# A spectral filter beside a token MLP on one core: the even half first, five buffer pairs in freed memory, single filter rows by small early transfers

## The chip, the cores and the metric

The kernel runs on one core of a Trainium2 chip. The metric is the device time of one launch in microseconds (us), the median of three runs. Beside it stands one profiled execution, from which all rows of the profile come.

## The reference

Two branches read the input `A_x` and its gate mixes them. The shapes are S = 2048 rows, D = 512 columns, F = 1792, all in bf16. `B_x` isn't read.

```python
x = A_x
g = sigmoid((x * gate_w).sum(-1, keepdims=True))
X = rfft2(x.astype(float32)) * (A_w_r + 1j * A_w_i)      # 2048 x 257
a = irfft2(X, s=(2048, 512)).astype(bfloat16)
h = layernorm(x)                                         # over D
u = gelu(einsum("bsd,sf->bdf", h, B_w1) + B_b1)          # tanh form
b = (einsum("bdf,fs->bds", u, B_w2) + B_b2).transpose(0, 2, 1)
return g * a + (1 - g) * b
```

## The kernel before

The function adds tasks (engine, estimated duration, emitting function, what it reads and writes, priority) to a planner, class `Plan`. `Plan.order` runs a list schedule over them by its own cost estimates and priorities, and the instructions are then emitted in that order. So each engine's order is fixed when the kernel is built, and it stands in the order of the program: an engine that waits holds up everything behind it. The entry `pk` of a transfer holds the number of its row pieces, their bytes, and on how many DMA engines the planner puts it.

Rows of `x` are numbered j = 4q + r; a tile of 128 rows belongs to each j.

*MLP.* Layer norm on VectorE and ScalarE (L473 to L531) makes `h`. The first product (L699, 224 matmuls of 512 columns) runs in an order of its own over 14 blocks of F, its GELU is L713 on ScalarE. The second product (L977, 14 matmuls for each j) is TensorE's filler until the end. For j under 14 ScalarE evicts it with gate and bias (L993); for the last two VectorE adds it in the tail (L1019).

*Spectral branch*, a two-dimensional transform in stages:

1. Along S: radix-4 sums of `x` on VectorE (L539 to L546), matmuls with `ta` (L556 to L559), evictions (L562), radix-4 sums (L569 to L576). The result is `X`, in two halves, index `lt`: even frequencies (0) and odd ones (1).
2. `radix4` (L595 to L608) on both halves: the odd half first, then the even half, whose first column is mended by a small chain (L620 to L638) and written at L646.
3. Along D: matmuls with `tb` (L664 to L667), evictions to `B` (L671), for the even half first.
4. Filter: `bfly` (L814, L815), multiplication by `W` (L822), `comb` (L827, L828), `ob` (L834 to L836); the Nyquist line apart (`nyq`, L795 to L798, and transfers through `s9` and `s8`). `W` and its mirror image are prepared before: `wt` is flipped by matmuls (L751), evicted (L755, L764), and the edges are taken at `wprep` (L771 to L775).
5. Inverse: `radix4` again (L595 to L611), matmuls (L883 to L890), evictions (L896, L898), folds (L906 to L919).
6. Last transform: for each j five matmuls (L957 to L961), an eviction to `eo` with the gate (L967), then for each pair a fold through `es` back into `eo` (L982 to L988) and an addition to the MLP's rows (L1007). `NEO` and `NES`, 2 each, are the pairs of buffers; a pair comes free after its L1007.

*Loads.* Nearly all are issued by SyncE (L310) in the planned order. `ld_W` loads, for the real and the imaginary filter, rows into `W` and `wt` in six transfers; eight single rows come in one transfer to one partition of `xp`, and `special` (L447 to L451) copies them on ScalarE to their places after that. `gw`, the gate's weights, is loaded ahead of the first `ld_W`; L724 multiplies `x` by it and L729 sums the product.

Of the kernel before, what the change touches and what calls it, by code (L numbers as in the profile page):

```python
# [23 lines left out]
L = 256  # L24
WL = 258
# [112 lines left out]
class Plan:  # L138
# [11 lines left out]
    def add(self, eng, dur, emit, reads=(), writes=(), prio=0.0, alloc=(), free=(), pk=None, after=()):  # L150
        t = Task()
        t.eng, t.dur, t.emit, t.prio = eng, dur, emit, prio
        t.alloc, t.free, t.pk = tuple(alloc), tuple(free), pk
        t.users, t.end, t.ready = [], None, 0.0
        deps = set(after)
        for k in reads:
            if k in self.last_w:
                deps.add(self.last_w[k])
            self.readers.setdefault(k, []).append(t)
        for k in writes:  # L160
            if k in self.last_w:
# [81 lines left out]
def tt(n):  # L243
    return 0.07 + n / 1920.0
# [19 lines left out]
def tiny(k):  # L264
    return 0.09 * k + 0.06
# [3 lines left out]
def kernel(  # L269
# [14 lines left out]
    V, A, T = nc.vector, nc.scalar, nc.tensor  # L284
# [7 lines left out]

    pool = ctx.enter_context(tc.tile_pool(name="sb", bufs=1))
    psum = ctx.enter_context(tc.tile_pool(name="ps", bufs=1, space=bass.MemoryType.PSUM))
    NEO, NES = 2, 2

    def sb(shape, dt, tag, bufs=1):
        return pool.tile(shape, dt, tag=tag, name=tag, bufs=bufs)
# [2 lines left out]
        return psum.tile(shape, dt, tag=tag, name=tag, bufs=bufs)  # L301

    NB = {"acc": 4, "fa": 2, "fb": 2}
    caps = {"wa": 1, "wb": 2, "xf": 2, "eo": NEO, "es": NES, **NB}
    pl = Plan(caps)
    add = pl.add
    t = {}

    def dma(out_ap, in_ap, eng=None):
        (eng or nc.sync).dma_start(out=out_ap, in_=in_ap)  # L310
# [34 lines left out]
    a0 = add("SP", 0.6, alloc_first, writes=["warm", "xs", "eps"], prio=-9)  # L345
# [82 lines left out]

    wsrc = (A_w_r, A_w_i)

    def ld_W(comp, pr):
        v = wsrc[comp].rearrange("(e c k) l -> c e k l", e=4, k=4)
        z = wsrc[comp].rearrange("(e h i n k) l -> n h k i e l", e=4, h=2, n=2, k=2)
        wz = lambda: t["xp"][0:1, 2048 + 8 * WL * comp:2048 + 8 * WL * (comp + 1)].rearrange("p (j l) -> p j l", j=8)
        for n, (key, dst, src, pk) in enumerate((
                ("wz", lambda: wz()[:, :, 0:257], wsrc[comp].rearrange("(u j w) l -> w u j l", u=1, j=8)[0], (8, 514, 8)),
                ("u0", lambda: t["wt"][0:64, comp, 0, :, 0:257], z[0, 1, 0], (256, 514)),
                ("u2", lambda: t["wt"][64:128, comp, 0, :, 0:257], z[1, 1, 0], (256, 514)),
                ("u1", lambda: t["wt"][:, comp, 1, :, 0:257], v[:, :, 3, :], (512, 514)),
                ("w0", lambda: t["W"][0:64, comp, 0, :, 0, 0:257], z[0, 0, 0], (256, 514)),  # L440
                ("w2", lambda: t["W"][64:128, comp, 0, :, 0, 0:257], z[1, 0, 0], (256, 514)),
                ("w1", lambda: t["W"][:, comp, 1, :, 0, 0:257], v[:, :, 1, :], (512, 514)))):
            add("SP", 0.5, lambda dst=dst, src=src: dma(dst(), src), writes=[(key, comp)], prio=pr + 0.1 * n, pk=pk, after=[a0])

        def special():
            W, u, w = t["W"], t["wt"], wz()
            A.copy(u[0:1, comp, 0, 0:2, 0:257], w[:, 5:8:2, 0:257])  # L447
            A.copy(u[0:1, comp, 0, 2, 0:257], w[:, 6, 0:257])
            A.copy(u[0:1, comp, 0, 3, 0:257], w[:, 0, 0:257])
            A.copy(W[0:1, comp, 0, 2:4, 0, 0:257], w[:, 1:4:2, 0:257])  # L450
            A.copy(t["wn"][:, comp, 0:257], w[:, 4, 0:257])  # L451
        add("ACT", 2.2, special, reads=[(k, comp) for k in ("wz", "u0", "u1", "u2", "w0", "w1", "w2")], writes=[("W", comp), ("wt", comp)], prio=4.5)

    for comp in range(2):
        ld_W(comp, 17 + 8 * comp)
        if comp == 0:
            load_wb(1)

# [179 lines left out]
        V.tensor_add(fx[:, 3, 1], sd[:, 1, 0, 1], sp[:, 2, 1])  # L638
    add("DVE", tiny(12), sp1, reads=["sp"], writes=["fx"], prio=0)

    for lt in (1, 0):
        pr = 3.0 if lt else 3.1
        radix4(lambda lt=lt: t["X"][:, lt].rearrange("p r c j l -> p r c (j l)"),
               lambda: t["xp"][:, 0:2048], lambda: t["st"][:, 0:2048], "xs", "st",
               dk + ([] if lt else ["sp"]), [("Z", lt, 0), ("Z", lt, 1)], pr, False)
    add("DVE", 0.15, lambda: V.tensor_copy(t["X"][:, 0, :, :, :, 0], t["fx"][:]), reads=["fx"],  # L646
        writes=[("Z", 0, 0), ("Z", 0, 1)], prio=3.1)

    def tbl(kind, c):
        tb = t["tb"]  # L650
# [290 lines left out]
    def tbuf(j):  # L941
        if "tb_" not in t:
            t["tb_"] = sb([P, NJ, 2, L], BF16, "x")
        return t["tb_"][:, j]

    LATE = 14
    groups = [range(0, 4), range(4, 8), range(8, 12), range(12, 14), range(14, 15), range(15, 16)]
    for grp in groups:
        for j in grp:
# [12 lines left out]
            add("PE", mm(*[129] * 5), i3, reads=[("z", 0), ("z", 1), "tg"], writes=[("i3", j)], prio=4, alloc=[tag])  # L962

            def i3ev(j=j):
                if j % 2 == 0:
                    t["eo", j // 2] = sb([P, 2, 2, L], BF16, "eo", NEO)
                A.activation(t["eo", j // 2][:, j % 2], t["i3", j][:], ActF.Copy, scale=t["g"][:, j:j + 1])  # L967
# [22 lines left out]

            if j < LATE:
                def yev(j=j):
                    A.activation(tbuf(j).rearrange("p h d -> p (h d)"), t["y", j, 0][:], ActF.Identity, bias=t["ombb2"][:, j:j + 1],  # L993
                                 scale=t["omg"][:, j:j + 1])
                add("ACT", act(512, 2), yev, reads=[("y", j, 0), "omg"], writes=[("o", j)], prio=1, free=["acc"], after=gates)
                if j % 2 == 0:
                    continue

                def es(j=j, fold=fold, quart=quart):
                    s, e = sb([P, 2, 4, P], BF16, "es", NES)[:], t["eo", j // 2]  # L1000
                    fold(e[:].rearrange("p j h d -> p (j h) d"), quart(e[:]), s)
                add("DVE", tiny(1) + 4 * tt(512), es, reads=[], writes=[("eo", j - 1), ("eo", j)], prio=4, alloc=["es"], free=["es"])

                def fin(j=j):
                    tbuf(j)
                    o = t["tb_"][:, j - 1:j + 1]
                    V.tensor_add(o, o, t["eo", j // 2][:])  # L1007
                add("DVE", tt(1024), fin, reads=[("eo", j - 1), ("eo", j)], writes=[("o", j - 1), ("o", j)], prio=4, free=["eo"])
            else:
                def es(j=j, fold=fold, quart=quart):  # L1010
                    e, s = t["eo", j // 2][:, j % 2], sb([P, 2, 4, P], BF16, "es", NES)[:, :, 0:2]
                    V.tensor_scalar_add(e[:, 0, 0:129], e[:, 0, 0:129], t["ombb2"][:, j:j + 1])
                    fold(e, quart(tbuf(j)[:, None]), s)
                add("DVE", tiny(1) + 4 * tt(256) + 0.15, es, reads=[("eo", j), "omg"], writes=[("o", j)], prio=4, alloc=["es"], free=["es", "eo"] if j % 2 else ["es"], after=gates)

                for n, cs in enumerate(parts):
                    def fin(j=j, n=n, cs=cs):
                        o = tbuf(j).rearrange("p h d -> p (h d)")[:, cs]
                        V.scalar_tensor_tensor(o, t["y", j, n][:, cs], t["omg"][:, j:j + 1], o, op0=Alu.mult, op1=Alu.add)  # L1019
                    add("DVE", d1(cs.stop - cs.start) + 0.1, fin, reads=[("y", j, n), "omg", ("o", j)], writes=[("of", j, n)], prio=1,  # L1020
                        free=[("acc", "fa")[n]])
# [42 lines left out]
```

## Time and profile before

| | us |
|---|---|
| median of three runs | 136.37 (135.94 to 136.87) |
| the profiled execution, its time | 136.38 |
| its span, first to last instruction | 134.5 |
| TensorE busy | 124.2 (92%) |
| VectorE busy | 112.4 (84%) |
| ScalarE busy | 88.9 (66%) |

The granted TensorE clock was 0.998 in the mean. The costliest groups are the second product (L977: 30.8 and 23.9 us) and the first (L699: 28.6, 16.9 and 9.4 us). TensorE's busy time is modelled, and a matmul that follows another is shown as overlapping it: a 512-column one lasts some 0.37 us by its row and follows its neighbour after about 0.22. Engines stand as PE (TensorE), DVE (VectorE), ACT (ScalarE) and SP (SyncE); SPq and ACTq are their queues of issued transfers.

### The profile page before, as it was taken

How to read it: one execution, taken by the hardware profiler on the slowest of the kernel's cores; microseconds unless marked ns; L12 is line 12 of the kernel's file. 1: busy time of each engine (PE TensorE's matmuls, PEld its weight loads, DVE VectorE, ACT ScalarE, POOL GpSimd, SP SyncE). 2: the span in 40 equal slices, each digit the busy share in tenths (PEclk: the TensorE clock that was granted, in tenths of full speed). 3: DMA queues.
4: the chain of work that ended last, by engine and by line, in shares of the span. 5: the costliest groups of instructions: out<-in, count | busy, mean ns of one | idle time of the engine just before them, and what ended most of it. 6: DMA issues, size and time to landing. Idle time of an engine off the chain costs nothing.

```text
span 134.5 us, 2134 instructions
## 1 busy us (share of the span) xinstructions
PE 124.2 (92%) x758; PEld 70.9 (53%) x771; DVE 112.4 (84%) x259; ACT 88.9 (66%) x185; POOL 0.2 (0%) x4
## 2 busy tenths in 40 slices
PE   6899999998999799999999999999999999999920
PEld 2345555554454475654454545555777576555810
DVE  2899999899999969309999999999769739797990
ACT  3798694979999599899991072223699375749300
POOL 0000000000000000000000000000000000000000
PEclk9999999999999999999999999999999999999999
DMA  4999999999999999980019500000000000214331
GB/s 125 330 352 364 358 373 345 314 175 237 327 266 185 325 410 409 401 328 10 0 17 392 217 0 0 7 0 2 0 0 5 0 0 0 104 55 161 156 117 41
DMA packets 17215, 23.22 MB, mean 173 GB/s; under 512 B 1040, under 2 KB 14644, under 8 KB 17204
## 3 DMA queue, kind: packets, MB, share of 16 engines
q1 hardware_dynamic: 16772, 22.63, 53.3%
q10 hardware_dynamic: 432, 0.46, 1.0%
q8 instruction: 6, 0.10, 0.3%
q14 instruction: 5, 0.04, 0.1%
HBM read 20.97 MB, written 2.10 MB: 172 GB/s over the span
## 4 chain that ended last, share of the span: by engine, by line
PE 42%; DMA 28%; DVE 13%; SPq 8%; ACT 4%; issue 2%; DVEq 0%; ACTq 0%
PE acc L977 21%; PE acc L699 12%; DMA wa<-in_B_w_dram 9%; SPq L310 8%; DMA gw<-in_gate_w_dram 8%; DMA W<-in_A_w_i_dram 6%; DMA wb<-in_B_w_dram 4%; ACT eo L967 3%; DVE eo L987 2%; DVE es L984 2%; DVE x L1007 2%; DVE es L983 2%; DVE eo L988 2%; PE fb L883 1%; PE fb L667 1%
## 5 line engine op out<-in xcount | busy, mean ns | idle before, releaser
L977 PE MATMUL acc<-gl,wb 128*128 128x512 bf16 (+1 forms) x124 | 30.8, 372 | 0.2
L699 PE MATMUL acc<-h,wb 128*128 128x512 bf16 x124 | 28.6, 379 | 0.5 <-ACT gl L713 0.4
L977 PE MATMUL acc<-gl,wa 128*128 128x512 bf16 (+1 forms) x94 | 23.9, 372 | 0.1
L993 ACT ACTIVATE x<-acc,ombb,omg 128x512 bf16<-128x512 f32 x14 | 10.7, 780 | 18.1 <-PE acc L977 18.1
L977 PEld LDWEIGHTS <-wb 128*128 128x128 bf16 x136 | 15.1, 114 | 10.7 <-DMA wb<-in_B_w_dram 0.8
L699 PEld LDWEIGHTS <-wb 128*128 128x128 bf16 x128 | 12.5, 98 | 14.0 <-DMA W<-in_A_w_r_dram 0.7
L699 PE MATMUL acc<-h,wa 128*128 128x512 bf16 x61 | 16.9, 379 | 1.0 <-DVE h L503 0.9
L977 PEld LDWEIGHTS <-wa 128*128 128x128 bf16 x102 | 11.3, 114 | 8.0 <-issue 0.2
L699 PEld LDWEIGHTS <-wa 128*128 128x128 bf16 x96 | 9.3, 98 | 9.9 <-issue 1.2
L562 ACT CAST X<-fa 128x512 bf16<-128x512 f32 x16 | 9.0, 580 | 2.5 <-PE fa L559 2.5
L473 DVE BATCH_NORM_STATS2 stats<-x 128x6 f32<-128x512 bf16 x13 | 8.9, 681 | 1.6 <-DMA x<-in_A_x_dram 1.6
L729 ACT ACTIVATE x<-x 128x512 bf16<-128x512 bf16 x16 | 9.9, 626 | 0.0
L967 ACT ACTIVATE eo<-fa,g 128x512 bf16<-128x512 f32 x8 | 5.5, 688 | 6.4 <-DVE x L1007 4.1
L699 PE MATMUL fb<-h,wa 128*128 128x512 bf16 x32 | 9.4, 379 | 0.0
L713 ACT ACTIVATE gl<-acc,b1f 128x512 bf16<-128x512 f32 x12 | 8.0, 691 | 1.4 <-PE acc L699 1.2
L531 ACT ACTIVATE h<-x,nmr,rstd 128x512 bf16<-128x512 bf16 x9 | 7.3, 814 | 1.5 <-DVE nmr L528 1.5
L967 ACT ACTIVATE eo<-fb,g 128x512 bf16<-128x512 f32 x8 | 5.5, 688 | 0.0
L982 DVE COPY es<-eo 128x8 bf16<-128x8 bf16 (+1 forms) x9 | 1.6, 182 | 4.4 <-ACT eo L967 4.3
L477 ACT ACTIVATE rstd<-mv,eps 128x1 f32<-128x1 f32 x16 | 4.7, 296 | 0.5 <-DVE rstd L527 0.4
L671 ACT CAST B<-fa 128x512 bf16<-128x512 f32 x8 | 4.8, 598 | 0.3 <-PE fa L667 0.3
L724 DVE TENSOR_TENSOR x<-x,gw 128x2048 bf16<-128x2048 bf16 x4 | 4.9, 1220 | 0.1
L671 ACT CAST B<-fb 128x512 bf16<-128x512 f32 x8 | 4.8, 601 | 0.0
(177 smaller groups left out, 240.5 us busy)
## 6 DMA issues: line engine op xcount, KB each, us to landing
wb<-in_B_w_dram SPq DMA_DIRECT2D x8, 512.0 KB, 8.0
wb<-in_B_w_dram SPq DMA_DIRECT2D x4, 1024.0 KB, 6.9
wa<-in_B_w_dram SPq DMA_DIRECT2D x3, 1024.0 KB, 9.4
wa<-in_B_w_dram SPq DMA_DIRECT2D x2, 768.0 KB, 6.8
out_dram<-x SPq DMA_DIRECT2D x3, 512.0 KB, 2.9
x<-in_A_x_dram SPq DMA_DIRECT2D x2, 512.0 KB, 6.7
wa<-in_B_w_dram SPq DMA_DIRECT2D x2, 384.0 KB
rot<-dft_ti SPq DMA_DIRECT2D x1, 736.5 KB, 7.4
```

What stands on the lines that cost most here:

```text
L310: (eng or nc.sync).dma_start(out=out_ap, in_=in_ap)
L473: V.bn_stats(out=t["stats"][:, j, :], in_=t["x"][:, j // 4, j % 4, :])
L531: add("ACT", act(512, 2), lambda j=j: A.activation(t["h"][:, j // 4, j % 4, :], t["x"][:, j // 4, j % 4, :], ActF.Identity, bias=t["nmr"][ ...
L562: add("ACT", act(512), lambda r=r, dq=dq: A.copy(t["X"][:, :, r, :, dq, :], t["pa", r, dq][:]), reads=[("pa", r, dq)], writes=[("X", r, dq ...
L671: A.copy(t["B"][:, lt, e, 2 * c:2 * c + 2, :].rearrange("p s (i b) -> p s i b", b=4), t["pb", lt, e, c][:].rearrange("p s b i -> p s i b"))
L699: T.matmul(t["u", ft][:], lhsT=w[:, j // 4, j % 4, c * P:(c + 1) * P], rhs=t["h"][:, j // 4, j % 4, :], start=(j == jorder[0]), stop=(j == ...
L713: gelus.append(add("ACT", act(512, 1), lambda ft=ft: A.activation(t["gl"][:, ft, :], t["u", ft][:], ActF.Gelu_apprx_tanh, bias=t["b1f"][:, ...
L724: add("DVE", tt(2048), lambda r=r: V.tensor_mul(t["x"][:, :, r, :], t["x"][:, :, r, :], t["gw"][:, None, :].to_broadcast([P, 4, D])), read ...
L729: A.activation(t["x"][:, q, r, :], t["x"][:, q, r, :], ActF.Copy, accum_out=t["glog"][:, 4 * q + r:4 * q + r + 1])
L967: A.activation(t["eo", j // 2][:, j % 2], t["i3", j][:], ActF.Copy, scale=t["g"][:, j:j + 1])
L977: T.matmul(t["y", j, n][:, cs], lhsT=w[:, o, 512 * q + r:512 * q + 512:4], rhs=t["gl"][:, ft, cs], start=(ft == 0), stop=(ft == NFT - 1))
L993: A.activation(tbuf(j).rearrange("p h d -> p (h d)"), t["y", j, 0][:], ActF.Identity, bias=t["ombb2"][:, j:j + 1], scale=t["omg"][:, j:j + 1])
```

## The change

Three edits, all in the main function.

- *Even half first.* The second stage runs `radix4` for the even half first and writes its mended column right after it. The priorities of the inverse `radix4` change so that the even half's stays ahead of the odd half's by less. Since the planner orders all engines, matmuls of the first product move about the later stages too.
- *Buffers.* `eo` and `es` are no longer tiles of their own. One tile `E` takes the memory of tag `X` (which `zz` held before): five pairs for evictions, one for the fold's intermediate, two (`ob`, `NOB`) for the fold's result. A pair now comes free after its fold; the addition reads `ob`.
- *Filter rows.* The eight-row transfers and `special` go. Each filter has five small transfers, of four, two, one, one and one rows, straight to partition 0 of `W`, `wt` and to `wn`. Their priorities put them early in the queue, between the loads of `x`, `w1` and `ta`. The two large transfers that had covered partition 0 start at partition 1: 63 rows in place of 64. A task without an instruction (`NOP`) ties the eleven loads to the readers.

In the changed program the ten small transfers stand on SyncE as follows: `w1` row 1 (half), small, `ta` row 1, `w1` row 1 (half), six small, `x` row 2, small, `ta` row 2, `w1` row 2, two small, `flip`, the two biases, `x` row 3.

```diff
-    NEO, NES = 2, 2
+    NEO, NOB = 5, 2
...
-    caps = {"wa": 1, "wb": 2, "xf": 2, "eo": NEO, "es": NES, **NB}
+    caps = {"wa": 1, "wb": 2, "xf": 2, "eo": NEO, "ob": NOB, **NB}
...
-    def ld_W(comp, pr):
...
-                ("wz", lambda: wz()[:, :, 0:257], wsrc[comp].rearrange("(u j w) l -> w u j l", u=1, j=8)[0], (8, 514, 8)),
-                ("u0", lambda: t["wt"][0:64, comp, 0, :, 0:257], z[0, 1, 0], (256, 514)),
...
-                ("w0", lambda: t["W"][0:64, comp, 0, :, 0, 0:257], z[0, 0, 0], (256, 514)),
...
-        def special():
...
-            A.copy(u[0:1, comp, 0, 0:2, 0:257], w[:, 5:8:2, 0:257])
-            A.copy(u[0:1, comp, 0, 2, 0:257], w[:, 6, 0:257])
-            A.copy(u[0:1, comp, 0, 3, 0:257], w[:, 0, 0:257])
-            A.copy(W[0:1, comp, 0, 2:4, 0, 0:257], w[:, 1:4:2, 0:257])
-            A.copy(t["wn"][:, comp, 0:257], w[:, 4, 0:257])
+    def ld_W(comp, pr, early):
...
+                (lambda: W()[0:1, 0, :, 0, 0:257].rearrange("p (a b) l -> p a b l", a=2), few, (4, 514, 4)),
+                (lambda: u()[0:1, 0, 0:2, 0:257], w.rearrange("(c w) l -> w c l", c=4)[256:257, 2:4], (2, 514, 2)),
+                (lambda: u()[0:1, 0, 2, 0:257], w[1536:1537, :], (1, 514, 1)),
+                (lambda: u()[0:1, 0, 3, 0:257], w[0:1, :], (1, 514, 1)),
+                (lambda: t["wn"][:, comp, 0:257], w[1024:1025, :], (1, 514, 1)),
+                (lambda: u()[1:64, 0, :, 0:257], z[0, 1, 0, 1:64], (252, 514, 9)),
...
+                (lambda: W()[1:64, 0, :, 0, 0:257], z[0, 0, 0, 1:64], (252, 514, 9)),
...
+        add("NOP", 2.0, lambda: None, reads=keys, writes=[("W", comp), ("wt", comp)])
...
-        ld_W(comp, 17 + 8 * comp)
+        ld_W(comp, 17 + 8 * comp, [2.3 + 1.1 * comp + 0.3 * n for n in range(5)])
...
-    for lt in (1, 0):
-        pr = 3.0 if lt else 3.1
+    for lt in range(2):
+        pr = 3.0 + 0.1 * lt
...
-        writes=[("Z", 0, 0), ("Z", 0, 1)], prio=3.1)
+        writes=[("Z", 0, 0), ("Z", 0, 1)], prio=3.0)
...
-        pr = 3.25 + 0.2 * lt
+        pr = 3.35 + 0.05 * lt
...
+    def epair(k):
+        if "E" not in t:
+            t["E"] = sb([P, 8192], BF16, "X")
+        return t["E"][:, 1024 * k:1024 * k + 1024].rearrange("p (j h d) -> p j h d", j=2, h=2)
+
+    def espair():
+        return t["E"][:, 1024 * NEO:1024 * NEO + 1024].rearrange("p (k m d) -> p k m d", k=2, m=4)
...
-                if j % 2 == 0:
-                    t["eo", j // 2] = sb([P, 2, 2, L], BF16, "eo", NEO)
-                A.activation(t["eo", j // 2][:, j % 2], t["i3", j][:], ActF.Copy, scale=t["g"][:, j:j + 1])
+                A.activation(epair(j // 2 % NEO)[:, j % 2], t["i3", j][:], ActF.Copy, scale=t["g"][:, j:j + 1])
...
-                    s, e = sb([P, 2, 4, P], BF16, "es", NES)[:], t["eo", j // 2]
-                    fold(e[:].rearrange("p j h d -> p (j h) d"), quart(e[:]), s)
+                    e = epair(j // 2 % NEO)
+                    fold(e.rearrange("p j h d -> p (j h) d"), quart(epair(NEO + 1 + j // 2 % NOB)), espair())
...
-                    V.tensor_add(o, o, t["eo", j // 2][:])
+                    V.tensor_add(o, o, epair(NEO + 1 + j // 2 % NOB))
```

More of the change, by code (lines that the diff above doesn't have):

```diff
@@ L429 @@
     wsrc = (A_w_r, A_w_i)
-    def ld_W(comp, pr):
[L432 to L435, printed above, removed]
-                ("wz", lambda: wz()[:, :, 0:257], wsrc[comp].rearrange("(u j w) l -> w u j l", u=1, j=8)[0], (8, 514, 8)),
-                ("u0", lambda: t["wt"][0:64, comp, 0, :, 0:257], z[0, 1, 0], (256, 514)),
-                ("u2", lambda: t["wt"][64:128, comp, 0, :, 0:257], z[1, 1, 0], (256, 514)),
-                ("u1", lambda: t["wt"][:, comp, 1, :, 0:257], v[:, :, 3, :], (512, 514)),
-                ("w0", lambda: t["W"][0:64, comp, 0, :, 0, 0:257], z[0, 0, 0], (256, 514)),
-                ("w2", lambda: t["W"][64:128, comp, 0, :, 0, 0:257], z[1, 0, 0], (256, 514)),
-                ("w1", lambda: t["W"][:, comp, 1, :, 0, 0:257], v[:, :, 1, :], (512, 514)))):
-            add("SP", 0.5, lambda dst=dst, src=src: dma(dst(), src), writes=[(key, comp)], prio=pr + 0.1 * n, pk=pk, after=[a0])
-        def special():
-            W, u, w = t["W"], t["wt"], wz()
-            A.copy(u[0:1, comp, 0, 0:2, 0:257], w[:, 5:8:2, 0:257])
-            A.copy(u[0:1, comp, 0, 2, 0:257], w[:, 6, 0:257])
-            A.copy(u[0:1, comp, 0, 3, 0:257], w[:, 0, 0:257])
-            A.copy(W[0:1, comp, 0, 2:4, 0, 0:257], w[:, 1:4:2, 0:257])
-            A.copy(t["wn"][:, comp, 0:257], w[:, 4, 0:257])
-        add("ACT", 2.2, special, reads=[(k, comp) for k in ("wz", "u0", "u1", "u2", "w0", "w1", "w2")], writes=[("W", comp), ("wt", comp)], prio=4.5)
@@ new lines, in ld_W @@
+    def ld_W(comp, pr, early):
+        w = wsrc[comp]
+        v = w.rearrange("(e c k) l -> c e k l", e=4, k=4)
+        z = w.rearrange("(e h i n k) l -> n h k i e l", e=4, h=2, n=2, k=2)
+        W, u = (lambda: t["W"][:, comp]), (lambda: t["wt"][:, comp])
+        few = w.rearrange("(c b a w) l -> w c a b l", c=2, b=2, a=2)[0:1, 0]
+        keys = []
+        for n, (dst, src, pk) in enumerate((
+                (lambda: W()[0:1, 0, :, 0, 0:257].rearrange("p (a b) l -> p a b l", a=2), few, (4, 514, 4)),
[4 more added lines that the diff above has]
+                (lambda: u()[1:64, 0, :, 0:257], z[0, 1, 0, 1:64], (252, 514, 9)),
+                (lambda: u()[64:128, 0, :, 0:257], z[1, 1, 0], (256, 514)),
+                (lambda: u()[:, 1, :, 0:257], v[:, :, 3, :], (512, 514)),
+                (lambda: W()[1:64, 0, :, 0, 0:257], z[0, 0, 0, 1:64], (252, 514, 9)),
+                (lambda: W()[64:128, 0, :, 0, 0:257], z[1, 0, 0], (256, 514)),
+                (lambda: W()[:, 1, :, 0, 0:257], v[:, :, 1, :], (512, 514)))):
+            keys.append(("Wl", comp, n))
+            add("SP", 0.5, lambda dst=dst, src=src: dma(dst(), src), writes=keys[-1:], prio=early[n] if n < 5 else pr + 0.1 * n, pk=pk, after=[a0])
+        add("NOP", 2.0, lambda: None, reads=keys, writes=[("W", comp), ("wt", comp)])
@@ L999, in es @@
                 def es(j=j, fold=fold, quart=quart):
-                    s, e = sb([P, 2, 4, P], BF16, "es", NES)[:], t["eo", j // 2]
-                    fold(e[:].rearrange("p j h d -> p (j h) d"), quart(e[:]), s)
-                add("DVE", tiny(1) + 4 * tt(512), es, reads=[], writes=[("eo", j - 1), ("eo", j)], prio=4, alloc=["es"], free=["es"])
+                    e = epair(j // 2 % NEO)
+                    fold(e.rearrange("p j h d -> p (j h) d"), quart(epair(NEO + 1 + j // 2 % NOB)), espair())
+                add("DVE", tiny(1) + 4 * tt(512), es, reads=[("eo", j - 1), ("eo", j)], writes=[("ob", j)], prio=4, alloc=["ob"], free=["eo"])
                 def fin(j=j):
@@ L1006, in fin @@
                     o = t["tb_"][:, j - 1:j + 1]
-                    V.tensor_add(o, o, t["eo", j // 2][:])
-                add("DVE", tt(1024), fin, reads=[("eo", j - 1), ("eo", j)], writes=[("o", j - 1), ("o", j)], prio=4, free=["eo"])
+                    V.tensor_add(o, o, epair(NEO + 1 + j // 2 % NOB))
+                add("DVE", tt(1024), fin, reads=[("ob", j)], writes=[("o", j - 1), ("o", j)], prio=4, free=["ob"])
             else:
                 def es(j=j, fold=fold, quart=quart):
-                    e, s = t["eo", j // 2][:, j % 2], sb([P, 2, 4, P], BF16, "es", NES)[:, :, 0:2]
+                    e, s = epair(j // 2 % NEO)[:, j % 2], espair()[:, :, 0:2]
                     V.tensor_scalar_add(e[:, 0, 0:129], e[:, 0, 0:129], t["ombb2"][:, j:j + 1])
                     fold(e, quart(tbuf(j)[:, None]), s)
-                add("DVE", tiny(1) + 4 * tt(256) + 0.15, es, reads=[("eo", j), "omg"], writes=[("o", j)], prio=4, alloc=["es"], free=["es", "eo"] if j % 2 else ["es"], after=gates)
+                add("DVE", tiny(1) + 4 * tt(256) + 0.15, es, reads=[("eo", j), "omg"], writes=[("o", j)], prio=4, free=["eo"] if j % 2 else (), after=gates)
                 for n, cs in enumerate(parts):
```

## Prediction

> **What bounds the kernel now.** I read the busy shares first, then who waited for whom, then the timelines of TensorE, VectorE and the SyncE queue, and the chain that ended last for the transfers.
>
> The page's busy shares and its row of DMA shares (tenths in 40 slices of 3.36 us), then the waits that matter (engine and line, what it waited for: us in all, times, longest):
>
> ```profile
> PE 124.2 (92%) x758; PEld 70.9 (53%) x771; DVE 112.4 (84%) x259; ACT 88.9 (66%) x185; POOL 0.2 (0%) x4
> ...
> DMA  4999999999999999980019500000000000214331
> ```
>
> ```profile
> DVE c L785 <- ACT B L671: 5.1, 1, 5.1
> ...
> ACT eo L967 <- DVE x L1007: 4.1, 4, 2.1
> ...
> PE fa L761 <- ACT W L755: 1.0, 1, 1.0
> ```
>
> TensorE is almost full, so the end can move only by TensorE's own waits and by what follows its last matmul. VectorE loses 5.1 us in one place, ScalarE 4.1 us for want of `eo` buffers.
>
> The timelines (start, duration, engine, line, tiles, idle before):
>
> ```profile
> 44.93 0.38 PE L751 MATMUL fa<-wt,flip 128*128 128x256 bf16 x2
> ...
> 47.19 0.20 PE L761 MATMUL fa<-wt,flip 128*128 128x8 bf16 x2 [1.00 <-ACT W L755]
> ...
> 48.14 0.22 PE L664 MATMUL fa<-tb,X 128*128 128x128 bf16 x1
> ...
> 127.50 1.04 PE L977 MATMUL fa<-gl,wb 128*128 128x256 bf16 x8
> ```
>
> ```profile
> 30.02 1.22 DVE L724 TENSOR_TENSOR x<-x,gw 128x2048 bf16<-128x2048 bf16 x1
> ...
> 46.98 0.69 DVE L608 TENSOR_TENSOR X<-st 128x1024 bf16<-128x1024 bf16 x1
> ...
> 130.72 0.48 DVE L1019 SCALAR_TENSOR_TENSOR x<-fa,omg,x 128x256 bf16<-128x256 f32 x1
> ```
>
> The last matmul group ends at 128.54; VectorE ends at 131.20, 2.66 later, because the folds of the last `eo` pairs run after TensorE is done. In the middle TensorE waits 1.00 us for ScalarE, whose copies of single filter rows stand in front of the evictions.
>
> The SyncE queue and the landings (chain pieces: start, length, what):
>
> ```profile
> 7.04 0.47 SPq L310 DMA_DIRECT2D x<-in_A_x_dram  x1
> ...
> 9.41 0.63 SPq L310 DMA_DIRECT2D b1b<-in_B_b_dram  x1
> 10.26 0.25 SPq L310 DMA_DIRECT2D b2b<-in_B_b_dram  x1
> 10.65 0.40 SPq L310 DMA_DIRECT2D x<-in_A_x_dram  x1
> ```
>
> ```profile
> 1.63 4.53 DMA wa<-in_B_w_dram
> ...
> 8.10 7.92 DMA wa<-in_B_w_dram
> ...
> 18.81 11.19 DMA gw<-in_gate_w_dram
> ...
> 36.55 8.59 DMA W<-in_A_w_i_dram
> ...
> 68.93 4.81 DMA wb<-in_B_w_dram
> ```
>
> `wa` issued at 1.63 lands at 6.16, and the next issue starts at 6.18; `wa` issued at 8.10 lands at 16.02, and the next starts at 16.03. Both times the waiting issue is the eighth after the landed one: eight transfers may be under way. `gw` lands at 30.00 and L724 starts at 30.02, so it has no slack. The DMA digits stay at 9 from 3 to 57 us: what is late early in this queue stays late.
>
> **The change, part by part.**
>
> *Five `eo` pairs and two `ob`.* Neither engine gets more work. The 4.1 us of ScalarE waits go, the evictions of the last transform run ahead, and the folds leave the tail. VectorE's work there is seven pairs at about 2.15 (1.54 fold and 0.61 add, from 112.09 to 113.63 and the next L1007) and 2.7 for the last two rows, 17.8 in all. Begun at about 107 it ends near 125, before TensorE. The order of the changed program has all folds ahead of the last three L1019 (L1025 there). After the last matmul there stay 0.1 and the 0.48 of one of them, 0.6 for 2.66: minus 2.06. If that cover were gone, the 1.4 of row 15's fold would come back. The memory is that of `zz`, free once L919 has run, which the last transform awaits anyway: nothing.
>
> *Filter rows by transfers.* The ten copies at L447 to L451 go, 4.9 us of ScalarE (0.61, 0.40, 0.40, 0.62, 0.40, twice), and with them the 1.00 us at L761. Ten narrow transfers come early, ahead of `x` rows 2 and 3, and two later ones of eight rows go. The price of a narrow issue isn't shown for one row; the rows of its stage are 0.63 (14 rows) and 0.25 (4), and 0.74 and 0.69 (8 rows) stand later, among full-width issues that also take 0.6 to 0.9. I take 0.44, the mean of the two in this stage, with 0.04 to the next; the range keeps 0.25 and 0.74.
>
> The queue then goes so: at 6.18 the first narrow, 6.66 `ta`, 7.04 `wa`, 7.52, 8.00, 8.48 narrow, 9.22 and 10.23 narrow (each held by the landing of the eighth before), 10.71 narrow, and `x` row 2 at 11.19, not 7.04. Half of the eight places now hold almost no bytes, so the engines run dry and the load pays its full latency: 2.25 (the 4.81 above less 2.56 of data) and 1.5 of data, landing at 14.94 for 13.39. Going on in the same way (narrow 11.97, `ta` 12.45, `wa` 12.90, two narrow, `flip`, two biases), `x` row 3 is issued at 16.1, not 10.65, and lands at 19.85 for 17.70: **2.15 late**. Both are in time for VectorE (first use at 16.28 and 22.00). From there the queue is full again, and all behind is 2.15 late: `gw` lands at 32.15.
>
> The big filter loads lose a row (63 for 64). The planner's entry puts such a load on 9 engines, 28 row pieces each in place of 16; a 64-row load took 0.65, so 12 more take 0.49. Three precede the load that the second flips (L751) await: 0 if spread evenly, 1.46 if the last engine is among the nine; which it is isn't shown, so I take 0.73.
>
> *Even half first.* No work is added. TensorE's first L664 now needs the even half and its fix (L646), and the order puts seven L699 more ahead of it (1.51 us). If the first L664 started at 48.14 + 1.51 = 49.65, TensorE would end as before. VectorE's 5.1 us go, and all later stages move up against the second product's matmuls, but since TensorE runs without a break this changes only which matmuls fill, not the sum.
>
> When does L664 start? The same matmuls precede the second flips: 44.93, and 0.4 for a `fb` bank that the earlier first flips must await from a GELU; then 3.5 of work (eight flips 0.87, twelve L699 2.6): 48.8 without lateness. By VectorE: 47.67, L646 0.3, `gw`'s 2.15: 50.1. By the filter: `W` lands at 45.14, the load before it 0.65 earlier, 44.49; with 2.15 and 0.73 it is 47.37, and 3.5 more give **50.87**. That is the latest, 1.22 over 49.65.
>
> **Sum.** 1.22 − 2.06 = −0.84, on the profiled execution's own 136.38 (its span 134.5 and 1.9 around it; the median is 136.37): **135.5**.
>
> [...]
>
> **Rivals.**
>
> *The lateness is swallowed.* Narrow issues are quick and no load runs dry. L664 starts at 48.8: −0.85 − 2.06, 133.5. For it: DMA-bound stretches hide small gaps, and the narrow transfers carry hardly any bytes. Against it: the eight places, which the two landings above show.
>
> *Nine engines throughout.* The full 1.46 in place of 0.73: L664 at 51.6, 136.3. For it, the planner's 9; against it, nothing shown on which engine lands last. [...]
>
> *Narrow issues dear (slower).* At 0.74 each the same walk issues `x` row 2 at 12.5 and row 3 at 18.0, which lands at 21.75: 4.05 late. The second flips then wait until 49.3, L664 starts at 52.8, 3.1 over 49.65: 137.5, and 138.2 with the nine engines. It is slower from the point where L664 starts after 51.71, that is, where that filter load lands after 48.2. For it: the two eight-row transfers to one partition took 0.74 and 0.69. Against it: they stood in a stage where all issues were long.
>
> *VectorE sets the third stage.* VectorE took 36.1 from L814 (60.66) to the end of the last L611 (96.77) without a wait. In the new order L814 starts 5.6 after L646 (L595 and L596 2.3, the filter's scaling 0.7, L600 to L608 2.4, L785 and L786 0.2), near 55.7, and the odd half's small steps (0.6) fall inside: 92.4. TensorE, by the matmuls that now stand between (0.215 for 512 columns), gets there 42.1 after its first L664, at 93.0. If VectorE is 1.6 later, TensorE waits 1.0: 136.5.
>
> **How the numbers follow.** The forecast, with narrow issues between 0.25 (1.55 late, 135.0) and 0.6, has 0.44; swallowed 0.28; nine engines 0.10; dear 0.12; VectorE 0.06. A measurement can tell about 1% (1.36 us). Faster by more than that is below 135.0: the swallowed case and a quarter of the forecast's, 0.39. Slower by more is above 137.7: 0.12. Within, 0.49. Range 133.2 to 137.6, from just under the swallowed case to the dear one; the forecast's own is 134.6 to 136.4.
>
> **What would show it.** Right: `x` row 2 issued near 11.2, `gw` landing near 32, a wait of some 2 us at L724, TensorE waiting 1.5 to 2.5 us at the second L751 or the first L664, no wait of ScalarE for `eo`, VectorE ending 0.6 after TensorE. Wrong: `gw` landing by 30.5 (swallowed), narrow issues above 0.6 us each (dear), or folds still running after the last matmul, which would take the gain away.

## The result and the profile after

The changed kernel takes 137.94 us (median of 4 runs, 137.59 to 138.16) where the kernel before took 136.39 (135.94 to 136.87) on the same chip: a ratio of 1.011, with a 95% interval of 1.007 to 1.015. It is 1.1% slower; 0.6% faster had been forecast. The profiled execution took 138.02, its span is 136.2.

The page's busy shares, and of its 40 slices the TensorE clock, the DMA shares and the bytes moved (a slice is now 3.40 us):

```profile
PE 126.4 (93%) x757; PEld 71.2 (52%) x771; DVE 112.5 (83%) x259; ACT 84.9 (62%) x175; POOL 0.2 (0%) x4
...
PEclk9999999999999986999999999999999999999998
DMA  4995898999999999998002850000000000333031
GB/s 116 350 341 177 248 303 277 359 345 184 194 341 273 171 275 406 408 414 356 22 0 19 362 237 0 2 5 2 0 0 0 5 0 0 156 156 137 22 115 39
```

ScalarE has lost its ten copies (88.9 to 84.9 us). Two things are new: a 5 and two 8s among the early DMA digits, with 177 to 303 GB/s in the four slices from 10.2 to 23.8 us, and a TensorE clock of 8 and 6 tenths from 47.7 to 54.5 us. The windows view (busy us and count of each engine, then the granted clock, the DMA share and GB/s) puts numbers on both, the kernel before ahead of the changed one:

```profile
10.20:23.80 13.60, 13.47 (x88) 7.43 (x88) 12.90 (x44) 10.14 (x23) 0.00 (x0) 1.00 1.08 360
```

```profile
10.20:23.80 13.60, 13.47 (x88) 7.39 (x88) 12.88 (x43) 9.94 (x23) 0.00 (x0) 1.00 0.79 251
46.71:50.12 3.41, 1.22 (x10) 1.00 (x11) 3.38 (x7) 0.79 (x2) 0.00 (x0) 1.00 1.09 226
50.13:53.54 3.41, 3.41 (x12) 1.26 (x10) 3.38 (x6) 2.05 (x6) 0.00 (x0) 0.50 1.01 392
53.54:56.95 3.41, 3.36 (x32) 2.44 (x31) 3.38 (x8) 2.66 (x6) 0.00 (x0) 1.00 1.02 408
```

In the first 13.6 us 109 GB/s are missing, 1.48 MB, which at 360 GB/s is 4.1 us of loading. The same view, two microseconds at a time, shows three dry places: 90 GB/s from 11 to 13 us, 185 from 14 to 16 and 154 from 20 to 22, where the kernel before moves 366, 354 and 356. The clock is exactly half from 50.13 to 53.54 us, for 3.41 us, and full on both sides. The SyncE queue in the same stretch, and the two landings on the chain of waits (start, length) that matter:

```profile
11.07 0.41 SPq L310 DMA_DIRECT2D x<-in_A_x_dram  x1
...
12.37 0.43 SPq L310 DMA_DIRECT2D wa<-in_B_w_dram  x1
...
14.89 0.39 SPq L310 DMA_DIRECT2D x<-in_A_x_dram  x1
16.74 0.36 SPq L310 DMA_DIRECT2D rot<-dft_ta  x1
19.13 0.37 SPq L310 DMA_DIRECT2D wa<-in_B_w_dram  x1
...
23.46 3.04 SPq L310 DMA_DIRECT2D gw<-in_gate_w_dram  x1
```

```profile
12.37 6.75 DMA wa<-in_B_w_dram
...
40.17 8.68 DMA wt<-in_A_w_i_dram
```

`x` row 2 goes out at 11.07 and row 3 at 14.89, but then the queue has only a `ta` part to add, and stands until 19.13: the next `wa` load waits for a place, that of the `wa` load issued at 12.37, which lands at 19.12. The trace tells what the eight places are: eight semaphores of the program, which the transfers of SyncE and ScalarE take in turn (these two loads both use number 99), and an issue starts only when the transfer that last used its semaphore has landed (here 19.13 after 19.12). The waits that follow:

```profile
DVE x L724 <- DMA gw<-in_gate_w_dram: 3.7, 1, 3.7
...
PE fa L751 <- DMA wt<-in_A_w_i_dram: 3.0, 1, 3.0
...
DVE c L785 <- ACT B L671: 1.2, 1, 1.2
```

VectorE's 5.1 us wait at L785 has become 1.2, ScalarE's waits for `eo` and TensorE's 1.00 us at L761 are gone; instead VectorE waits 3.7 us for `gw` and TensorE 3.0 us for the filter load of the second flips. TensorE's and VectorE's timelines:

```profile
48.90 0.39 PE L751 MATMUL fa<-wt,flip 128*128 128x256 bf16 x2 [2.96 <-DMA wt<-in_A_w_i_dram]
...
49.79 1.58 PE L699 MATMUL acc<-h,wb 128*128 128x512 bf16 x4
...
51.26 3.00 PE L699 MATMUL acc<-h,wb 128*128 128x512 bf16 x8
54.09 0.22 PE L664 MATMUL fa<-tb,X 128*128 128x128 bf16 x1
...
132.14 1.04 PE L983 MATMUL fa<-gl,wb 128*128 128x256 bf16 x8
```

```profile
131.69 0.48 DVE L1025 SCALAR_TENSOR_TENSOR x<-acc,omg,x 128x256 bf16<-128x256 f32 x1 [0.78 <-PE acc L983]
133.22 0.48 DVE L1025 SCALAR_TENSOR_TENSOR x<-fa,omg,x 128x256 bf16<-128x256 f32 x1 [1.04 <-PE fa L983]
```

Eight L699 matmuls take 3.00 us where eight take 1.89 at full clock (a row of the experiments, below): in this stretch they follow each other every 0.43 us. The last row shows VectorE waiting for TensorE at the end, so the folds no longer make a tail: VectorE ends at 133.70, TensorE at 133.18.

### The profile page after: what moved, and what is told of

Same layout as the page of the kernel before. It is cut to its first block, busy times and chain, and to the rows that moved or that the text cites. A ratio compares the mean times of both kernels' runs of the same rounds, so it can differ in the third digit from the quotient of the medians.

```text
span 136.2 us, 2134 instructions
## 1 busy us (share of the span) xinstructions
PE 126.4 (93%) x757; PEld 71.2 (52%) x771; DVE 112.5 (83%) x259; ACT 84.9 (62%) x175; POOL 0.2 (0%) x4
## 4 chain that ended last, share of the span: by engine, by line
PE 47%; DMA 30%; SPq 10%; DVE 10%; issue 1%
PE acc L983 29%; DMA wa<-in_B_w_dram 11%; SPq L310 10%; DMA wb<-in_B_w_dram 8%; DMA wt<-in_A_w_i_dram 6%; PE acc L699 5%; DMA s<-X 4%; DVE st L822 2%; DVE xp L822 2%; PE fa L883 1%; PE fb L667 1%; PE fa L667 1%; PE fb L883 1%; PE fa L983 1%; DVE X L795 1%
## 5 line engine op out<-in xcount | busy, mean ns | idle before, releaser
L699 PE MATMUL acc<-h,wb 128*128 128x512 bf16 x124 | 31.1, 395 | 0.5 <-ACT gl L713 0.4
L983 PE MATMUL acc<-gl,wa 128*128 128x512 bf16 (+1 forms) x93 | 23.2, 372 | 0.2
L699 PEld LDWEIGHTS <-wb 128*128 128x128 bf16 x128 | 12.8, 100 | 14.3 <-issue 2.4
L699 PE MATMUL acc<-h,wa 128*128 128x512 bf16 x61 | 17.1, 382 | 0.4 <-DVE h L503 0.2
L699 PEld LDWEIGHTS <-wa 128*128 128x128 bf16 x96 | 9.2, 98 | 10.1 <-issue 1.2
L699 PE MATMUL fb<-h,wa 128*128 128x512 bf16 x32 | 9.4, 379 | 0.0
L973 ACT ACTIVATE X<-fa,g 128x512 bf16<-128x512 f32 x8 | 5.6, 697 | 1.1 <-PE fa L969 1.1
L973 ACT ACTIVATE X<-fb,g 128x512 bf16<-128x512 f32 x8 | 5.6, 695 | 0.0
L854 ACT CAST s<-fa 8x512 bf16<-8x512 f32 x1 | 0.6, 574 | 7.8 <-PE fa L852 7.8
L360 PE MATMUL fa<-xp 128*128 128x512 bf16 x9 | 4.0, 631 | 1.2 <-DVE xp L321 1.2
```

Source lines behind the costliest of these rows:

```text
L699: T.matmul(t["u", ft][:], lhsT=w[:, j // 4, j % 4, c * P:(c + 1) * P], rhs=t["h"][:, j // 4, j % 4, :], start=(j == jorder[0]), stop=(j == ...
L973: A.activation(epair(j // 2 % NEO)[:, j % 2], t["i3", j][:], ActF.Copy, scale=t["g"][:, j:j + 1])
L983: T.matmul(t["y", j, n][:, cs], lhsT=w[:, o, 512 * q + r:512 * q + 512:4], rhs=t["gl"][:, ft, cs], start=(ft == 0), stop=(ft == NFT - 1))
```

## The experiments

Theory 1: the filter rows' transfers are what costs. They make all that stands behind them in the queue late, TensorE waits, and behind its wait its clock falls. Theory 2: the new order itself costs, since TensorE's first L664 must wait for the even half. In the table, landings and starts are those of each profiled execution, in us; "filter load" is the 128-row load that the second flips await, "wait" TensorE's for it, "tail" VectorE's end after TensorE's.

| kernel | gw lands | filter load lands | wait | clock near 50 us | first L664 | tail | time (median) | ratio to before, 95% |
|---|---|---|---|---|---|---|---|---|
| before | 30.00 | 44.37 | none | full | 48.14 | 2.66 | 136.4 | |
| changed | 33.77 | 48.86 | 3.0 | half | 54.09 | 0.52 | 137.9 | 1.011 (1.007 to 1.015) |
| e1 buffers alone | 29.78 | 44.00 | none | full | 47.67 | 1.54 | 135.0 | 0.988 (0.984 to 0.993) |
| e2 even half first alone | 31.35 | 45.68 | 0.5 | full | 51.93 | 0.52 | 133.7 | 0.983 (0.972 to 0.994) |
| e3 filter rows alone | 32.61 | 48.49 | 2.6 | half | 52.23 | 2.65 | 139.7 | (none) |
| e4 changed, old filter rows | 30.39 | 47.10 | 2.1 | half | 54.64 | 0.52 | 133.9 | 0.981 (0.972 to 0.989) |
| e5 changed, wait filled | 34.68 | 48.29 | filled | full | 52.94 | 0.52 | 136.2 | 1.000 (0.997 to 1.003) |
| e6 rows spread later | 29.87 | 44.80 | 0.6 | full | 50.75 | 0.52 | 133.8 | 0.981 (0.974 to 0.988) |
| e7 rows on GpSimd's queue | 29.73 | 44.58 | 1.1 | full | 50.95 | 0.52 | 134.0 | 0.985 (0.978 to 0.992) |
| e8 the same, 64-row loads | 31.39 | 44.71 | none | full | 49.65 | 2.93 | 134.7 | 0.989 (0.985 to 0.993) |
| e9 wait half filled | 33.32 | 48.93 | 1.5 | full | 52.48 | 0.52 | 136.0 | 0.995 (0.990 to 0.999) |
| e10 wait filled by a third | 33.98 | 49.40 | 1.9 | full | 52.96 | 0.52 | 136.9 | 0.995 (0.991 to 1.000) |
| e11 e6 with the old buffers | 29.49 | 44.70 | 0.3 | full | 50.65 | 0.52 | 133.9 | 0.978 (0.973 to 0.982) |

The runs come from several chips, so each ratio is to the kernel before on the same chip. The profiled execution of e4 is the longest of its four (137.84); the other three took 133.5 to 134.0 and the ratio is theirs, while the mean of all four is 134.8. The ratio of e1 leaves out its longest of ten (136.51), that of e10 its two longest of eight (137.37 and 138.05). For e3 no interval can be given; its four executions took 137.09, 139.54, 139.76 and 140.38.

### One part at a time: e1 to e4

e1, the kernel before with the `eo` edit alone:

```
-    NEO, NES = 2, 2
+    NEO, NOB = 5, 2
...
-                    t["eo", j // 2] = sb([P, 2, 2, L], BF16, "eo", NEO)
+                A.activation(epair(j // 2 % NEO)[:, j % 2], ...)
```

> The kernel before with the five eo pairs alone. Both theories: the folds leave the tail, VectorE ends some 0.6 us after TensorE in place of 2.66, no ScalarE wait for eo is left, and the time is 134.3 (2.1 less than before). If the folds only move in front of TensorE's own work, the time stays near 136.

135.0, 1.2% less, so the buffers help by themselves; but the tail is 1.54 us, not 0.6: 1.1 of the 2.06 that was put on them. The waits view and VectorE's timeline of e1:

```profile
DVE X L988 <- ACT X L973: 2.8, 1, 2.8
```

```profile
109.53 0.19 DVE L988 COPY X<-X 128x8 bf16<-128x8 bf16 x1 [2.75 <-ACT X L973]
...
127.88 1.14 DVE L1025 SCALAR_TENSOR_TENSOR x<-acc,omg,x 128x512 bf16<-128x512 f32 x2
128.93 0.47 DVE L1025 SCALAR_TENSOR_TENSOR x<-fa,omg,x 128x256 bf16<-128x256 f32 x1
```

The folds can't begin at 107: the first needs ScalarE's evictions of the last transform and starts at 109.53. From there VectorE works without a wait of note until 129.40, and TensorE is done at 127.86.

e2, the kernel before with the order alone:

```
-    for lt in (1, 0):
-        pr = 3.0 if lt else 3.1
+    for lt in range(2):
+        pr = 3.0 + 0.1 * lt
...
-        writes=[("Z", 0, 0), ("Z", 0, 1)], prio=3.1)
+        writes=[("Z", 0, 0), ("Z", 0, 1)], prio=3.0)
...
-        pr = 3.25 + 0.2 * lt
+        pr = 3.35 + 0.05 * lt
```

> The kernel before with the even half first alone (old filter rows, old buffers). Theory 1 (the narrow row transfers are what costs): gw lands at 30.0 as before, VectorE's 5.1 us wait at L785 goes, the first L664 starts between 49.0 and 50.5, the time is 136.4 within 0.8. Theory 2 (the new order itself costs, because TensorE's first L664 must wait for the even half and its fix): the first L664 starts after 51.5 and the time is 138 or more.

133.7: faster than either theory had it, though its first L664 starts at 51.93 (the longest of its four executions, 135.36; the others took 133.4 to 133.7). The reason is the tail. The waits view and VectorE's last row of e2:

```profile
ACT eo L967 <- DVE x L1007: 5.2, 4, 2.1
```

```profile
130.56 0.48 DVE L1019 SCALAR_TENSOR_TENSOR x<-fa,omg,x 128x256 bf16<-128x256 f32 x1 [1.04 <-PE fa L977]
```

With two `eo` pairs ScalarE still waits 5.2 us, but VectorE is done with its folds before TensorE's last matmuls, because its last L919 ends at 105.33 and not 107.11 while TensorE, in this longest execution, ends 2 us later than before. The order alone takes the tail away; e11, below, has the same old buffers and the same 0.52.

e3, the kernel before with the ten narrow transfers and the 63-row loads (the new `ld_W` in place of the old one, nothing else):

> The kernel before with the filter rows by ten early narrow transfers alone. Theory 1: gw lands near 33.8 in place of 30.0, VectorE waits 3.5 to 4 us at L724, the second flips at L751 start near 48.5, TensorE's clock dips behind that wait as in the changed kernel, the time is 138.5 to 140.5. Theory 2 (the order costs, the transfers only look late): within 0.8 of 136.4.

139.7 by the median, inside theory 1's range; but one of the four executions took 137.09, under it, so the time alone settles little. In the trace `gw` lands at 32.61, 1.2 us earlier than theory 1 expected; the filter load, at 48.49, is as late as it expected, and TensorE's clock is half from 48.14 to 51.55 us, behind the wait.

e4, the changed kernel with the old `ld_W` and its copies:

> The changed kernel with the old loading of the filter rows (even half first and five eo pairs kept). Theory 1: gw at 30.0, second flips near 45.3, no dip of TensorE's clock near 50 us, the 1.0 us wait for ScalarE's single-row copies back at the eighth-row flips; 134.3 within 0.7. Theory 2: 136 or more, with a first L664 after 51.5.

133.9, 2% under the kernel before. So the filter rows cost 4.1 us in the changed kernel (137.94 less 133.85; the ratios, 1.011 and 0.981, say the same), and theory 2 falls: with the new order and without the rows the kernel is faster than before. The expected "no dip" failed in one of its four executions, the profiled one, where the filter load landed late (47.10). TensorE's timeline and the windows of it:

```profile
47.15 0.39 PE L751 MATMUL fa<-wt,flip 128*128 128x256 bf16 x2 [2.06 <-DMA wt<-in_A_w_i_dram]
...
49.75 0.20 PE L761 MATMUL fa<-wt,flip 128*128 128x8 bf16 x2 [1.33 <-ACT W L755]
```

```profile
46.25:49.66 3.41, 1.26 (x9) 0.90 (x10) 2.05 (x4) 1.94 (x5) 0.00 (x0) 1.00 1.06 320
49.66:53.07 3.41, 3.32 (x10) 1.22 (x10) 1.75 (x5) 2.77 (x9) 0.00 (x0) 0.50 1.02 404
```

Two waits close together, 2.06 and 1.33 us, went with a half clock of again 3.41 us there.

### The clock by itself: e5, e9 and e10

```
-                    pw = t["pw", comp, lt, a] = ps([P, 2, L], F32, tag, 2)
+                    pw = t["pw", comp, lt, a] = ps([P, 2, L], F32, tag, 2); [T.matmul(pw[:].rearrange("p i l -> p (i l)"), lhsT=t["flip"][:, 0:P], rhs=t["tb"][:, 0:512], start=True, stop=True) for _ in range(14 if (comp, lt, a) == (1, 1, 0) else 0)]
```

> The changed kernel with 14 matmuls of 512 columns put ahead of the second flips, 3.0 us at 0.215 each, that write into the bank that the flips overwrite; nothing else in the order differs. Theory 1 (TensorE's 3 us wait makes its clock fall, and that is a loss of its own): the wait is filled, the dip of the granted clock near 50 us goes, the matmuls behind the flips are 0.215 apart, the first L664 comes near 52.3 in place of 54.1, and the time is 1.5 to 2 us under the changed kernel's 137.94, at 136.2, in every run. Theory 2 (the dip has another cause, or the matmuls behind it were not on the path): 137.9, or more by what the 14 matmuls overrun.

136.2, as theory 1 had it, and all ten executions lie between 135.87 and 136.87 with a mean clock of at least 0.996, where the changed kernel's four had 0.985 to 0.987. A half clock of 3.41 us takes 0.0125 from that mean, so none of the ten had one. TensorE's timeline:

```profile
46.02 3.19 PE L749 MATMUL fa<-tb,flip 128*128 128x512 bf16 x14
49.04 0.38 PE L751 MATMUL fa<-wt,flip 128*128 128x256 bf16 x2
...
50.84 1.89 PE L699 MATMUL acc<-h,wb 128*128 128x512 bf16 x8
52.94 0.23 PE L664 MATMUL fa<-tb,X 128*128 128x128 bf16 x1 [0.22 <-DVE X L646]
```

The second flips start no earlier (49.04 for 48.90), the load is as late as ever, and 14 matmuls that compute nothing make the kernel 1.7 us faster (137.94 less 136.2; by the ratios, 1.011 and 1.000, 1.5 us). They only keep TensorE busy. The first L664 came 0.6 us later than expected; 0.22 of it is a wait for L646; `gw` had landed at 34.68, 0.9 later than in the changed kernel's profile.

e9 and e10 put 7 and 4 such matmuls in place of 14.

> The changed kernel with 7 instead of 14 matmuls ahead of the second flips, 1.5 us; some 1.6 us of TensorE's wait stay. Theory A (the clock falls when TensorE has nothing to do for some 2 us or more in one piece; waits of 1.2 and 1.8 us left it alone, 2.2 and more did not): no dip, 136.2 as with 14. Theory B (any wait above about 1 us together with the short ones behind it is enough): the dip near 50 us is there and the time is near 137.9.

> The changed kernel with 4 matmuls ahead of the second flips, 0.9 us; some 2.3 us of TensorE's wait stay, in one piece. Theory A: the dip is there, near 137.9; if it isn't, the limit lies above 2.3 us in one piece and the shorter waits that went with a dip were helped by those behind them.

```profile
48.97 0.38 PE L751 MATMUL fa<-wt,flip 128*128 128x256 bf16 x2 [1.50 <-DMA wt<-in_A_w_i_dram]
```

```profile
49.45 0.38 PE L751 MATMUL fa<-wt,flip 128*128 128x256 bf16 x2 [1.94 <-DMA wt<-in_A_w_i_dram]
```

(Both expectations count a wait from where the last matmul's work ends, 0.16 us more than the rows: their 1.2, 1.8 and 2.2 us are 1.05 in e7, 1.65 at L761 in e2 and 2.06 in e4.) With 1.5 us of wait left (e9) there is no dip in any of six executions: theory A. In e10 the profiled wait was 1.94, so 2.3 was not tested; it left the clock alone. Seven of eight executions ran at a mean clock of at least 0.997 and one, of 138.05, at 0.984; how long that one waited isn't recorded.

The length of one wait is not what decides. In the three profiles with a fall near 50 us the half clock lasts 3.41 us, and the full clock before it lasted a whole number of such steps: 13 in the changed kernel (from 5.75 us to 50.13), 12 in e3, 13 in e4. In the one step just ahead of the fall TensorE was busy for 1.22 us in the changed kernel, 1.26 in e4 (their windows above) and 1.23 in e3 (44.73 to 48.14), so idle for about 2.2 of 3.41. In e9 the whole wait falls into one step as well, and the clock stays:

```profile
47.32:50.73 3.41, 1.91 (x14) 1.20 (x13) 3.38 (x6) 1.35 (x3) 0.00 (x0) 1.00 1.07 256
```

So e4's two waits count together, as far as they lie in one step (0.90 and 1.25 us). The ends of the runs narrow the limit: in the kernel before the step from 126.97 to 130.38 has 1.57 us of busy time and no fall behind it, in e4 that from 131.58 to 134.98 has 1.41 and a fall. In these traces, then, the fall comes at 2.0 us of idle time within a step and not yet at 1.8. Where the steps begin differs from one execution to the next (5.75 us in the changed kernel, 5.29 in e4, 7.18 in e3, 6.36 in e9), so the same wait can lie in one step or be split over two; that this explains e10's one execution is not shown.

### The rows elsewhere: e6, e7, e8 and e11

e6 keeps the ten transfers on SyncE's queue, but behind `x` and `w1`, between wide loads:

```
-        ld_W(comp, 17 + 8 * comp, [2.3 + 1.1 * comp + 0.3 * n for n in range(5)])
+        ld_W(comp, 17 + 8 * comp, [10.05 + 12 * comp + 0.1 * n for n in range(5)])
```

> The changed kernel with the ten narrow transfers issued later on the same queue: the five of the first part between the four wide loads of wb and gw, the five of the second between the next four of wb. Theory 1a (what costs is that the narrow ones hold places among the few wide loads of the early stage): gw lands by 31.5, the filter load for the second flips by 46.5, no wait of TensorE above 2 us there, 133.5 to 134.5. Theory 1b (the narrow transfers cost the same wherever they stand): gw near 32 and that load near 48.5 as in the changed kernel, 136.5 to 138.

133.8, theory 1a. In the windows view the early stretch is full again, and on TensorE's timeline the wait is short:

```profile
10.20:23.80 13.60, 13.43 (x88) 7.51 (x88) 12.86 (x44) 10.11 (x24) 0.00 (x0) 1.00 1.08 362
```

```profile
44.85 0.39 PE L751 MATMUL fa<-wt,flip 128*128 128x256 bf16 x2 [0.64 <-DMA wt<-in_A_w_i_dram]
```

The same ten transfers, each still 0.2 to 0.7 us to issue, cost 4.2 us less when they go out 11 to 13 us later (the second five 22 us later). The planner also moved some flips in TensorE's order when the rows' times changed, here and in e7, so a little of the time may be the order's; `gw` and the early stretch don't depend on it.

e7 issues them from GpSimd at its beginning (`nc.gpsimd` in place of `nc.sync` for n < 5):

> The changed kernel with the ten narrow transfers issued on GpSimd's queue, at its beginning, and no longer on SyncE's; the loads of 63 rows stay. Theory 1 (issue time and places in SyncE's queue are the price, not the narrow data): x row 2 issued near 7 us again, gw lands near 30.5, the filter load for the second flips near 45.3 (0.9 late by the loads on nine engines), 133 to 134.5. Theory 2 (the narrow data itself, on one or two engines, slows the wide loads): gw after 32, 136 or more.

134.0, theory 1: 362 GB/s in the same stretch, `gw` at 29.73, the filter load at 44.58. So the rows may be moved early, if not by SyncE. Two things differ at once here: SyncE's issue time and the places in its queue are both free of the rows (`x` row 2 goes out at 6.88, where the changed kernel has 11.07). e6, where the issue time is paid and the rows go as before, speaks for the places among the early loads as the price; the two were not parted further.

e8 goes back to loads of 64 rows, with the narrow rows behind them on GpSimd's queue:

```
-                (lambda: u()[1:64, 0, :, 0:257], z[0, 1, 0, 1:64], (252, 514, 9)),
+                (lambda: u()[0:64, 0, :, 0:257], z[0, 1, 0], (256, 514)),
...
+            bt_[n] = add(..., after=[a0] if n > 4 else [bt_[8]] if n == 0 else [bt_[5]])
```

> As the run before, but the loads of 63 rows are loads of 64 rows again, and the narrow rows follow on GpSimd's queue after the 64-row load that they overwrite. If the loads on nine engines cost 0.9 us on the way to the second flips, that filter load lands near 44.5 and the time is 0.5 to 1 us under that run, where nothing else binds; if they cost nothing, the two are within 0.4. The narrow rows now land late, some 2 us after their load; if the flips of the even half wait for them, the time is above that run's.

134.7, 0.7 above e7 (the intervals overlap): neither of the first two cases, and on the side of the third. The filter load lands at 44.71, about e7's 44.58, though `gw` landed 1.7 later; landings move by more than 1 us from one execution to the next (`gw` between 33.32 and 34.68 in the changed kernel, e5, e9 and e10, which load alike), so the price of nine engines isn't settled by this pair. Nor do the two differ in the loads alone: with the rows late, the planner puts the second flips behind the L664s, at 57.53, so in e8 nothing waits for the filter load, and its "none" in the table says nothing of it. What e8 loses at its end comes from these late flips: VectorE waits where it did not in e7 (waits view of e8),

```profile
DVE W L771 <- ACT W L764: 1.9, 1, 1.9
```

and its last L919 starts at 107.84 against 103.08, so that the tail is back (2.93).

e11 is e6 without the buffers:

> The kernel before with the even half first and the filter rows by narrow transfers spread among the wide loads of wb, but with the two eo buffers of before. If the new order alone takes the folds out of the tail, as the run with the even half first alone suggests, the buffers are worth nothing here: 133.7 within 0.5, as with them, and VectorE ends some 0.6 us after TensorE. If the buffers are worth their 2 us: 135.5 or more.

133.9, against 133.8 with them: behind the new order five `eo` pairs are worth nothing that can be measured, as e2 (133.7) and e4 (133.9) had shown. e2, e4, e6, e7 and e11 all beat both kernels, by 1.5 to 2.2% of the kernel before, and lie too close to rank.

## Why the prediction was wrong

*The walk down the queue was right as far as `x` row 2.* The mean of the ten narrow issues was 0.45 (0.44 taken), and `x` row 2 went out at 11.07 (11.19) and landed at 14.52 (14.94). Row 3 went out earlier than walked, at 14.89 (16.1), and yet landed later, at 20.93 (19.85): 3.2 late, not 2.15. The load ahead of it had lost the time: `wa`, 0.75 MB, issued at 12.37 with mostly small transfers around it, landed at 19.12, where the same load before landed at 16.01, 3.1 earlier. The walk let the engines run dry once, ahead of `x` row 2. They ran short a second time: the first packets of this `wa` load move at about 14.3 us, but the rate from 14 to 16 is 185 GB/s.

*"From there the queue is full again, and all behind is 2.15 late" is the first step that failed.* The `wa` load's successor, the eighth after it, had to wait for its place until 19.13. So the engines ran short a third time, at 154 GB/s from 20 to 22 us: this load landed at 24.39, 4.1 late (20.25 before), and `gw` 3.8 late. The term of 2.15 was mis-sized by 1.6, of which 1.1 was there at `x` row 3. The 4.1 us of missing bytes between 10.2 and 23.8 us are the same loss counted on the other side.

*Nine engines.* All behind `gw` went from 3.8 late to 4.5 at the filter load (48.86 for 44.37), 0.7 more; 0.73 was taken, an estimate from the planner's entry of 9. In the trace such a load reports nine arrivals (the one issued at 26.54: one at 27.08, right after its issue, and nine from 31.79 to 33.89) and a 64-row load sixteen. But landings of other kernels with the same loads scatter by more than that (from `gw` to the filter load 13.6 us in e5, 15.6 in e9; 14.4 before), so the agreement may be luck. That nine engines carry it throughout, the rival of 1.46, is neither shown nor ruled out.

*"3.5 more give 50.87" is the second.* The work from the second flips to the first L664 was priced at full clock. It took 5.19 us (48.90 to 54.09), 1.7 more, because the clock was half for 3.41 us behind the wait, which is 1.7 us of work. No rival had this, although the wait itself was forecast ("TensorE waiting 1.5 to 2.5 us"). e5 shows it to be the cause: with TensorE kept busy, 1.5 to 1.7 us come back, although the second flips start as late as ever. The two steps together, 1.5 and 1.7, are the 3.2 us by which the first L664 missed.

*The point from which it is slower held.* It was given as a filter load later than 48.2 or a first L664 after 51.71; they came at 48.86 and 54.09. The cause given with it, dear issues, was not what happened: they took 0.45 in the mean, not 0.74.

*The base of 49.65 held.* From there to TensorE's end it would have been 78.9; the changed kernel took 79.1, and the others with the new order between 77.9 and 79.1.

*The 2.06 of the tail came, from the wrong part.* The tail is 0.52 (0.6 predicted). But e2 gets it by the order alone, and e1 only 1.1 by the buffers alone, since the folds start at 109.5 and not at 107 and end at 127.9, with the three additions of the MLP's last rows still behind them. That all later stages move up "changes only which matmuls fill, not the sum" was the slip: what VectorE gains by the order (1.8 us at the last L919 in e2) was not counted in the tail, which depended on it. That the sum had the tail right was luck. A further 0.8 had not been seen: from VectorE's end to the span's end it took 3.3 us before and 2.5 after. The last store was issued 0.49 us after VectorE's end before and 0.03 after; in e3, whose last two additions come as close together as before, it was 0.06 and the whole 2.6. So this part isn't shown to come from the change.

*The sum, as measured.* First L664 4.4 over 49.65, 0.2 in what follows, −2.1 of tail, −0.8 behind it: +1.7 on 136.38, 138.1 against 138.02.

## What to carry to other kernels

A small transfer took one of the queue's eight places here as a large one did (the first narrow one from 6.14 to 9.53 us, the `wa` load before it in that place from 1.63 to 6.12): put such transfers where the transfers around it are wide enough to keep the engines busy without those places (e6: 362 GB/s from 10.2 to 23.8 us, against 251), and walk the queue until the lateness has stopped growing, not until the first landing that looks in time. In these traces TensorE's clock was half for 3.41 us behind a step of that length with about 2.2 us of idle time: price that half clock (1.7 us of work here) where a forecast wait leaves as much of a step idle, or fill the wait with matmuls that compute nothing. When one part of a change moves an engine's whole schedule up, ask which later cost depends on that schedule before a second part is given credit for it.

## What the chip showed that was not expected

- After a TensorE wait of 2.96 us the granted clock was 0.50 from 50.13 to 53.54 us, then full; matmuls of 512 columns were 0.43 us apart in it, 0.215 outside. The first flips behind the wait still ran at full clock, and the fall came 1.2 us after work had begun again; in e3 it was there before the first flips (48.14 against 48.54).
- In these traces the fall follows the idle time within one 3.41 us step: about 2.2 us ahead of the three falls near 50 us (TensorE was busy for 1.22 to 1.26 us of these steps), and 2.0 at the end of e4, while 1.5 in e9 and 1.8 at the end of the kernel before left the clock alone.
- Ten narrow transfers on GpSimd's queue took 0.5 to 0.7 us each to issue and left the early loads at 362 GB/s; on SyncE's queue at the same early stage they cost 109 GB/s for 13.6 us.
